# Filler products cut into quarters beside the attention scores, with drains and a new table

## The chip, the cores and the metric

The kernel runs on one core of a Trainium2 chip. The metric is the device time of one execution in microseconds, the median of several. A core has five engines that work side by side and wait for each other by semaphores: TensorE (PE in the profile, its weight loads PEld), VectorE (DVE), ScalarE (ACT), GpSimd (POOL) and SyncE (SP), which issues most DMAs. TensorE has an array of 128 by 128 cells; a matmul can be given a part of it, here 32 of its columns with all 128 rows ("128*32" in the profile) or 32 of its rows with all 128 columns ("32*128").

## What is computed

Two layers, each an attention block and an MLP block on x of 2048 by 512, with the same weights in both layers:

```python
def _A_ref(x, wqkv, wo):            # H = 32 heads of Dh = 16
    qkv = (x @ wqkv).reshape(B, S, 3, H, Dh).transpose(2, 0, 3, 1, 4)
    q, k, v = qkv[0], qkv[1], qkv[2]
    scores = jnp.einsum("bhqd,bhkd->bhqk", q, k) * (Dh ** -0.5)
    p = _softmax(scores, axis=-1)
    o = jnp.einsum("bhqk,bhkd->bhqd", p, v)
    return o.transpose(0, 2, 1, 3).reshape(B, S, D) @ wo

def _B_ref(x, w1, w2):              # Dff = 1792
    return jnp.maximum(x @ w1, 0) @ w2

x = x + _A_ref(_layernorm(x), A_wqkv, A_wo)
x = x + _B_ref(_layernorm(x), B_w1, B_w2)
# and both once more
```

The output is bfloat16. Most of the work is 2 x 32 x 2048 x 2048 exponentials.

## The kernel before

**Slots.** The scores come in blocks of 128 keys by 512 queries of one head. Four heads lie side by side in a tile of keys and queries, each in 32 of the 128 partitions; the number of such a group, g from 0 to 3, is the row group of the array in which the block's scores are computed. A slot takes three blocks (`W = 3`), of three different groups where it can, writes their scores with three matmuls (L2231) into one of two PSUM buffers `ps_s` of three banks, and has ScalarE take the exponential of all three, or of two (L2249). There are 1366 slots, one exponential instruction each. Where two are taken, VectorE makes the third block's exponential from an integer word (L1750), and GpSimd adds a constant to two such blocks at a time, up and down (L1811); the block is then summed in three parts.

**Columns.** Each exponential block is multiplied by the values (L1404), into one of two accumulators, `ps_o` or `ps_f`. Head g writes 32 partitions, so these matmuls take 128 rows and 32 columns, and four of them with different g run side by side, a round. `v_round` (L1488) issues a round; where it has no block for some of the four groups of columns, it may put a filler cell there (`grid_column`, L501).

**Fillers.** All else that TensorE has to do, the projections and both MLP matmuls, is cut into groups of products (`mm_group`, L681). A product multiplies 128 rows by 128 columns by 512, and a group adds 4 of them into a bank (14 in the second MLP matmul), which VectorE then reads. A group of this kind is a *grid*: each product is four cells of 32 columns (`grid_cell`, L463, its matmul on L467), and a full unit (`grid_unit`, L484) issues four. The bank is whichever of `ps_o` and `ps_f` the sums of the attention do not hold.

**The order.** The program is written out in order by a planner in Python. It keeps a clock for each engine (`now_pe`, `now_dve`, `now_pool`, `now_act`), advances it by a fixed cost for each instruction (`MM = 216`, `SWITCH = 105` for a change between rows and columns, and so on, in ns), and fills each slot up to a limit (L2190) with rounds and filler units: `pace` says how many filler units a slot ought to do, `owed` how many it is behind, `margin` how long before ScalarE needs them the scores ought to be done. Only the order of instructions comes out of this; the engines still wait for each other by semaphores. `take_unit` (L2021) picks the blocks of a slot. `rule` holds the planner's settings, and `RULES` changes some of them from a given slot on. `STARTS` forces or forbids a slot's third for VectorE, `MORE` adds to what is owed, `SLIP` moves a slot's limit.

At the head of a slot's scores stands

```python
        for _ in range(times):
            pe_run("s", 1, s_ready, TUCK[now[0][0]["w"]])
            for a, (sg, kb, g) in sorted(zip(place, now), key=in_turn):
```

so that the planner counts one matmul's time for all three.

Of the kernel before, what the change touches and what calls it, by code (L numbers as in the profile page):

```python
# [26 lines left out]
def kernel(  # L27
# [10 lines left out]
    nc = tc.nc  # L38
# [13 lines left out]
    QS = 512  # L52
# [18 lines left out]
    GROUP = 2  # L71
# [17 lines left out]
    SMALL, W1, TRANSPOSE = (600.0, 1600.0), (430.0, 3000.0), (1400.0, 3600.0)  # L89
# [6 lines left out]
    STARTS, MORE, SLIP = {13: 0, 16: 1, 40: 0, 23: 1, 30: 0, 33: 0, 56: 0, 53: 0, 54: 1, 47: 0, 103: 1, 127: 1, 141: 1, 184: 1, 252: 1, 254: 0, 313: 0, 342: 0, 353: 0, 344: 1, 370: 1, 382: 1, 419: 1, 451: 0, 453: 1, 456: 0, 444: 0, 508: 0, 509: 1, 538: 0, 532: 1, 547: 0, 566: 1, 578: 0, 585: 1, 592: 0, 642: 1, 654: 0, 646: 0, 641: 1, 670: 0, 696: 1, 682: 0, 719: 0, 715: 1, 728: 1, 737: 1, 772: 0, 819: 1, 834: 0, 857: 0, 844: 1, 855: 0, 854: 1, 873: 0, 886: 1, 905: 1, 918: 1, 938: 1, 929: 0, 976: 0, 1000: 0, 1006: 1, 1001: 0, 1025: 0, 1031: 1, 1092: 0, 1128: 1, 1151: 1, 1166: 1, 1172: 0, 1250: 0, 1260: 0, 1266: 1, 1263: 0, 1340: 0, 1326: 0, 1364: 0, 1362: 0, 1366: 0, 1371: 0}, {9: -1.0, 13: 2.0, 7: 2.0, 38: 1.0, 39: 2.0, 32: 2.0, 52: 2.0, 41: -1.0, 48: 1.0, 126: 1.0, 153: 2.0, 187: -1.0, 204: 2.0, 221: -1.0, 237: 1.0, 229: -1.0, 264: 2.0, 265: -1.0, 266: 1.0, 300: 2.0, 281: 1.0, 285: 1.0, 308: 1.0, 320: 2.0, 318: -1.0, 327: -1.0, 355: 2.0, 378: -1.0, 371: 1.0, 372: 2.0, 388: 2.0, 396: -1.0, 391: -1.0, 437: 1.0, 495: 2.0, 538: 2.0, 543: 2.0, 574: 2.0, 603: 2.0, 659: 1.0, 684: -1.0, 685: 1.0, 711: -1.0, 807: 1.0, 804: 2.0, 813: -1.0, 828: 1.0, 836: 2.0, 832: 2.0, 855: 2.0, 879: 2.0, 861: -1.0, 862: -1.0, 896: 1.0, 897: 1.0, 899: 2.0, 956: -1.0, 948: 1.0, 961: 2.0, 987: -1.0, 1008: 1.0, 1035: -1.0, 1079: 1.0, 1089: 1.0, 1100: -1.0, 1099: -1.0, 1110: 2.0, 1164: 1.0, 1263: -1.0, 1267: 2.0, 1277: 2.0, 1299: 1.0, 1336: 2.0, 1365: -1.0, 1375: 1.0, 1371: 2.0}, {3: 120.0, 56: -200.0, 102: 60.0, 133: -200.0, 175: -200.0, 194: 120.0, 184: -200.0, 196: 120.0, 259: 60.0, 245: 60.0, 241: -200.0, 321: -200.0, 325: -200.0, 322: 60.0, 357: -200.0, 370: -200.0, 366: 120.0, 377: -200.0, 384: -200.0, 385: -200.0, 390: 120.0, 419: 120.0, 434: 216.0, 436: 120.0, 435: 60.0, 497: -200.0, 517: 60.0, 523: 60.0, 530: -200.0, 521: -200.0, 551: -200.0, 549: 60.0, 559: 216.0, 574: -200.0, 634: 60.0, 666: -200.0, 691: 216.0, 692: 60.0, 689: -200.0, 718: -200.0, 722: -200.0, 726: -200.0, 740: 120.0, 818: 120.0, 828: 60.0, 825: 60.0, 822: -200.0, 891: -200.0, 922: 60.0, 932: -200.0, 931: 120.0, 946: 60.0, 951: -200.0, 945: 60.0, 1011: 216.0, 1013: -200.0, 1002: 216.0, 1034: 60.0, 1062: 216.0, 1064: 120.0, 1067: 60.0, 1097: 60.0, 1114: 60.0, 1131: 120.0, 1220: -200.0, 1218: 60.0, 1242: 216.0, 1279: 60.0, 1289: -200.0, 1294: 216.0, 1296: 216.0, 1312: 60.0, 1307: -200.0, 1308: 60.0, 1323: 216.0, 1353: -200.0, 1361: -200.0, 1365: -200.0, 1370: -200.0}  # L96
# [6 lines left out]
        "haste": 2.0, "margin": 130.0, "join": -1.0, "room": 0, "keep": 2, "wide": 1, "share": 4,  # L103
    }
    RULES = {1: {'rounds': 3, 'hold': 2, 'closing': 3, 'fill': 2000.0}, 21: {'young': 5}, 41: {'easy': 1.0, 'keep': 1}, 61: {'old': 3, 'spare': 6, 'rounds': 4, 'fill': 3000.0, 'over': 200.0, 'young': 6, 'pressed': 6, 'closing': 6}, 101: {'least': 0.5, 'spare': 20, 'margin': 160.0, 'far': 4}, 121: {'near': 8, 'pressed': 2, 'soon': 1400.0, 'old': 4}, 141: {'keep': 2, 'late': 4.0, 'ahead': 8.0, 'unit': 360.0}, 161: {'pressed': 6, 'hold': 3, 'spare': 6, 'least': 0.8, 'far': 4, 'soon': 2000.0, 'haste': 1.6, 'near': 4}, 181: {'wide': 1, 'haste': 3.0}, 201: {'hold': 4, 'backlog': 3000.0}, 221: {'keep': 3, 'easy': 1.4, 'haste': 2.0, 'far': 2}, 241: {'haste': 3.0, 'full': 4}, 261: {'margin': 100.0}, 281: {'late': 3.0}, 301: {'late': 99.0, 'least': 0.5, 'unit': 400.0, 'easy': 1.0, 'keep': 2, 'young': 5, 'pace': 1.0, 'full': 3}, 321: {'keep': 3, 'easy': 2.0}, 341: {'young': 3}, 361: {'haste': 2.0}, 401: {'young': 6, 'unit': 360.0}, 421: {'pace': 1.0, 'slack': 1300.0, 'over': 0.0, 'eager': 0, 'partial': 3, 'backlog': 2200.0, 'closing': 3, 'cap': 3.0}, 441: {'pace': 1.15, 'young': 6, 'rounds': 4, 'keep': 2, 'calm': 3.0, 'far': 2, 'soon': 1400.0, 'unit': 320.0}, 461: {'slack': 1300.0, 'fill': 2000.0, 'closing': 3, 'unit': 360.0}, 481: {'unit': 400.0, 'soon': 2000.0, 'rounds': 4, 'late': 4.0, 'eager': 0, 'least': 0.5, 'fill': 2000.0, 'haste': 1.6}, 541: {'late': 2.0, 'least': 0.8}, 561: {'keep': 2, 'near': 10, 'margin': 100.0, 'hold': 2}, 581: {'ahead': 12.0, 'closing': 6, 'slack': 800.0, 'full': 5}, 601: {'ahead': 8.0, 'cap': 6.0}, 661: {'near': 12, 'ahead': 12.0, 'closing': 3, 'pace': 1.15}, 701: {'spare': 10}, 721: {'haste': 2.0, 'rounds': 4, 'near': 10, 'over': 0.0, 'pace': 1.3, 'eager': 1, 'keep': 2, 'young': 5}, 761: {'hold': 4, 'partial': 3, 'pace': 0.7, 'cap': 3.0, 'closing': 0, 'wide': 2, 'join': -1.0, 'near': 10}, 801: {'late': 99.0}, 821: {'eager': 1, 'calm': 1.2}, 841: {'keep': 2, 'cap': 3.0, 'least': 0.8, 'share': 4, 'backlog': 2200.0, 'room': 0, 'near': 6, 'haste': 1.3}, 861: {'backlog': 3000.0}, 881: {'share': 2}, 901: {'full': 3}, 921: {'eager': 1, 'rounds': 4, 'least': 0.5, 'partial': 3, 'margin': 60.0, 'haste': 1.6, 'full': 3, 'pace': 1.5}, 941: {'over': 60.0, 'late': 99.0}, 961: {'partial': 2, 'near': 12, 'cap': 10.0, 'far': 3, 'easy': 1.2, 'slack': 1300.0, 'soon': 1000.0, 'full': 3}, 981: {'rounds': 3, 'backlog': 2200.0}, 1021: {'wide': 0, 'cap': 6.0}, 1061: {'over': 200.0, 'spare': 10}, 1081: {'spare': 20, 'haste': 1.3, 'over': 120.0, 'slack': 300.0, 'easy': 1.6, 'backlog': 1500.0, 'room': 0, 'pace': 0.85}, 1101: {'soon': 1400.0, 'unit': 320.0}, 1121: {'far': 2, 'slack': 300.0, 'fill': 3000.0, 'ahead': 1.0, 'calm': 2.0, 'haste': 2.0, 'hold': 2, 'cap': 3.0}, 1161: {'unit': 400.0, 'far': 3}, 1241: {'near': 12, 'haste': 1.3, 'keep': 2, 'eager': 0}, 1261: {'full': 5}, 1301: {'keep': 2, 'cap': 3.0}, 1321: {'rounds': 3, 'room': 8}, 1341: {'fill': 2000.0, 'spare': 10}, 1361: {'fill': 2000.0, 'over': 60.0, 'hold': 3, 'unit': 400.0, 'eager': 0, 'ahead': 8.0, 'calm': 3.0, 'pressed': 6}}
# [232 lines left out]
    mode = [None]  # L338
    grid = [None]
# [46 lines left out]
    def pe_run(kind, units, ready=0.0, extra=0.0):  # L386
        start = pe_start(kind, ready)
        now_pe[0] = start + units * MM + extra
        mode[0] = kind
        streams.append((start, now_pe[0]))  # L390
# [51 lines left out]
    def start_group(g):  # L442
# [8 lines left out]
        if g["grid"]:  # L451
            n = len(g["grid"]["mms"])
            grid[0] = dict(
                g["grid"], b=bank(), ready=ready, cols=[deque(range(n)) for _ in range(4)],
                begun=[False] * 4,
            )
            cur.extend((1.0, grid_unit, ready if n == 0 else 0.0, "f") for n in range(n))
            return
# [4 lines left out]
    def grid_cell(c, g):  # L463
        G = grid[0]
        lhsT, rhs = G["mms"][c]
        cols = slice(32 * g, 32 * g + 32)
        nc.tensor.matmul(  # L467
            G["b"][cols], lhsT[:, cols], rhs, start=not G["begun"][g], stop=not G["cols"][g],
            tile_position=(0, 32 * g), skip_group_check=True,
        )  # L470
        G["begun"][g] = True

    def grid_settle():
        G = grid[0]
        n = max(len(x) for x in G["cols"])
        while len(cur) > n:
            cur.pop()
# [6 lines left out]
    def grid_unit():  # L484
# [3 lines left out]
        grid_settle()  # L488

# [20 lines left out]
    def do_piece():  # L510
        c, fn, ready, kind = cur.popleft()
        pe_run(kind, c, ready)
        fn()
        owed[0] -= c
# [12 lines left out]
    def fill_pe(limit, floor=0.0, most=99):  # L527

        done = 0
        while owed[0] > floor and done < most:  # L530
            limit_now = limit if owed[0] < 5.0 or not hurry[0] else now_pe[0] + 1000.0
# [286 lines left out]
    def ln_rows(tag, tt, n, i):  # L818
# [11 lines left out]
        if i == n - 1:  # L830
# [26 lines left out]
            for k in range(n):  # L857
                task(
                    420, lambda k=k: apply(k),
# [1636 lines left out]
```

## Time and profile before

| | |
|---|---|
| median of 3 runs | 1368.37 us (1368.16 to 1368.6) |
| the profiled execution | 1367.16 us |
| its span, first to last instruction | 1365.4 us |
| TensorE's granted clock | 1.0 |
| exponentials, L2249, ScalarE | 1319.0 us busy |
| filler cells, L467, TensorE | 5000 matmuls |
| GpSimd busy | 58% |

The page of the profile gives each engine's busy time and its share of the span, then the chain of work that ended last. Matmuls are pipelined: a matmul's record is longer than the time after which the next can start, so a busy share near 100% says that work follows on work, not that the array is used to its peak. Timelines give the start, the length, the engine, the line, the operation, what is written from what, and how many such instructions are merged. A "q" behind an engine's name (PEldq) is its sequencer.

### The profile page before, as it was taken

The numbers are of one execution on the slowest core, as the hardware profiler recorded it, in microseconds if no ns is written. First come the engines' busy times: TensorE is split into PE (matmuls) and PEld (weight loads), VectorE is DVE, ScalarE is ACT, GpSimd is POOL, SyncE is SP. The second block draws the span as 40 slices with busy tenths as digits, with TensorE's granted clock in tenths as the row PEclk, the third lists the DMA queues.
The fourth block names the chain that finished last, engine by engine and source line by source line (L and its number), as shares of the span: only waits on it lengthen the run. The fifth ranks groups of instructions, "written<-read, shape, count | busy, mean of one in ns | idle before, by whom it ended". The sixth has DMA issues, their size and how long they took to land.

```text
span 1365.4 us, 49106 instructions
## 1 busy us (share of the span) xinstructions
PE 1327.1 (97%) x20780; PEld 468.5 (34%) x20782; DVE 1161.8 (85%) x2024; ACT 1333.1 (98%) x1437; POOL 789.0 (58%) x1324
## 2 busy tenths in 40 slices
PE   8999999999999999999999999999999999999998
PEld 3222222222222222222222222222234444545665
DVE  7898889878998789997899877998888888988883
ACT  8999999999999999999999999999999999999994
POOL 3357766666666566675466654565446565666440
PEclk9999999999999999999999999999999999999999
DMA  6200112112024120321203100002312401324112
GB/s 152 66 2 18 26 33 42 42 43 41 11 52 107 33 57 14 95 53 41 49 21 90 29 29 13 26 16 49 102 43 49 113 21 41 78 45 99 31 39 37
DMA packets 166669, 66.63 MB, mean 49 GB/s; under 512 B 137617, under 2 KB 161617, under 8 KB 166449
## 3 DMA queue, kind: packets, MB, share of 16 engines
q1 hardware_dynamic: 159920, 57.89, 17.5%
q0 software_dynamic: 5568, 5.15, 2.0%
q8 instruction: 162, 2.65, 0.8%
q10 hardware_dynamic: 960, 0.46, 0.1%
q14 instruction: 59, 0.48, 0.1%
HBM read 38.80 MB, written 4.19 MB: 31 GB/s over the span
## 4 chain that ended last, share of the span: by engine, by line
PE 56%; ACT 33%; DVE 8%; issue 2%; DMA 1%; POOL 0%; SPq 0%; POOLq 0%; DVEq 0%; ACTq 0%
PE ps_s L2231 19%; ACT e L2249 15%; PE ps_f L1404 9%; PE ps_o L1404 9%; PE ps_o L467 8%; PE ps_f L467 7%; ACT xx L2249 7%; DVE words L1750 3%; ACT w L2249 3%; ACT wv L2249 2%; ACT val L2249 2%; ACT ktl L2249 1%; ACT words L2249 1%; ACT ktp L2249 1%; PE ps_o L716 1%
## 5 line engine op out<-in xcount | busy, mean ns | idle before, releaser
L2249 ACT ACTIVATE e<-ps_s 128x1024 bf16<-128x1024 f32 (+1 forms) x627 | 695.2, 1190 | 5.9 <-PE ps_s L2231 2.2
L1750 DVE TENSOR_SCALAR words<-ps_s 128x512 int16<-128x512 f32 x864 | 580.8, 685 | 94.9 <-PE ps_s L2231 81.5
L1811 POOL INT64_ADD words<-words x581 | 356.0, 622 | 258.9 <-DVE words L1750 205.4
L2231 PE MATMUL ps_s<-q,ktp 32*128 32x512 bf16 (+2 forms) x4110 | 478.2, 331 | 14.9 <-ACT e L2249 7.5
L2231 PEld LDWEIGHTS <-ktp 32*128 32x128 bf16 x4393 | 151.5, 91 | 452.1 <-issue 445.0
L2249 ACT ACTIVATE xx<-ps_s 128x1024 bf16<-128x1024 f32 x283 | 300.9, 1128 | 1.4 <-PE ps_s L2231 1.1
L2231 PE MATMUL ps_s<-q,ktl 32*128 32x256 bf16 (+2 forms) x1359 | 197.6, 289 | 0.9 <-ACT ktp L2249 0.3
L1404 PEld LDWEIGHTS <-vaug 128*32 128x32 bf16 x4686 | 116.4, 95 | 150.0 <-issue 130.7
L2249 ACT ACTIVATE w<-ps_s 128x1024 bf16<-128x1024 f32 x111 | 118.1, 1106 | 0.0
L1404 PE MATMUL ps_f<-e,vaug 128*32 128x512 bf16 (+2 forms) x830 | 111.6, 322 | 0.4 <-DVE q L977 0.2
L1404 PE MATMUL ps_o<-e,vaug 128*32 128x512 bf16 (+2 forms) x768 | 105.9, 335 | 0.3 <-DVE ht L1236 0.2
L1750 DVE TENSOR_SCALAR xx<-ps_s 128x512 int16<-128x512 f32 x128 | 86.4, 683 | 16.4 <-PE ps_s L2231 14.0
L1404 PE MATMUL ps_o<-words,vaug 128*32 128x512 bf16 (+2 forms) x647 | 92.1, 348 | 0.7 <-DVE u L1260 0.3
L1404 PE MATMUL ps_f<-words,vaug 128*32 128x512 bf16 (+2 forms) x559 | 89.5, 373 | 0.8 <-DVE vaug L953 0.5
L1404 PEld LDWEIGHTS <-val 128*32 128x32 bf16 x2744 | 73.3, 96 | 44.9 <-issue 34.8
L2231 PEld LDWEIGHTS <-ktl 32*128 32x128 bf16 x1359 | 61.4, 92 | 56.6 <-issue 55.0
L1404 PE MATMUL ps_o<-words,vscaled 128*32 128x512 bf16 (+2 forms) x514 | 78.7, 331 | 1.5 <-POOL words L1811 1.1
L1811 POOL INT64_ADD words<-xx x83 | 50.7, 620 | 49.0 <-DVE xx L1750 29.6
L2249 ACT ACTIVATE val<-ps_s 128x1024 bf16<-128x1024 f32 x67 | 73.6, 1129 | 0.0
L467 PE MATMUL ps_o<-w,ht 128*32 128x512 bf16 x896 | 73.0, 383 | 0.0
L2249 ACT ACTIVATE wv<-ps_s 128x1024 bf16<-128x1024 f32 x65 | 71.7, 1123 | 0.6 <-PE ps_s L2231 0.5
L1404 PE MATMUL ps_o<-xx,vaug 128*32 128x512 bf16 (+1 forms) x325 | 70.2, 382 | 0.6 <-DVE vaug L1258 0.5
(318 smaller groups left out, 2651.4 us busy)
## 6 DMA issues: line engine op xcount, KB each, us to landing
w<-in_B_w_dram SPq DMA_DIRECT2D x144, 128.0 KB
w<-in_B_w_dram SPq DMA_DIRECT2D x35, 256.0 KB
q<-xn SPq DMA_DIRECT2D x38, 64.0 KB
wv<-in_A_wqkv_dram SPq DMA_DIRECT2D x8, 256.0 KB
away<-xx SPq DMA_DIRECT2D x8, 256.0 KB
xx<-away SPq DMA_DIRECT2D x8, 256.0 KB
out_dram<-xx SPq DMA_DIRECT2D x15, 128.0 KB
xx<-in_A_x_dram SPq DMA_DIRECT2D x14, 128.0 KB
```

The source lines that it names most:

```text
L467: nc.tensor.matmul(G["b"][cols], lhsT[:, cols], rhs, start=not G["begun"][g], stop=not G["cols"][g], tile_position=(0, 32 * g), skip_group ...
L716: nc.tensor.matmul(out[cols], lhsT[:, cols], rhs, start=i % k == 0, stop=i % k == k - 1, tile_position=(0, 32 * g), skip_group_check=True,)
L1404: nc.tensor.matmul((ps_f, ps_o)[sg["bank"]][32 * g : 32 * g + 32, 0 : sg["w"]], values[:, 4 * sg["T"] + g, 2 * e : 2 * e + 32], rhs, start ...
L1750: first = nc.vector.tensor_scalar(out=words[which][:, half * QS : (half + 1) * QS], in0=src, scalar1=EXP_BIAS, scalar2=THIRD, op0=ALU.add, ...
L1811: ins = nc.gpsimd.int64_add(of(part).bitcast(I64), of("lin").bitcast(I64), by)
L2231: score = nc.tensor.matmul(b[:, a : a + sg["w"]], kt[32 * g : 32 * g + 32, kc : kc + P], q_home(sg["q"])[32 * g : 32 * g + 32, sg["e"], 0 ...
L2249: ex = nc.scalar.activation(out=eb[:, 0 : place[m]], in_=b[:, 0 : place[m]], func=ACTF.Exp, scale=1.0 / (LOG2E * UNIT),)
```

## The change

A filler product may now be cut the other way, into four quarters of 32 rows, each with all 128 columns, that add into the same bank. Just ahead of the first of a slot's scores, `beside_scores` looks for a row group that none of the slot's blocks uses, and issues one quarter there, so that it runs beside the scores. It opens a group for this if none is open. A new product is cut only if at least `rest` times the pace (at most 1) products remain uncut in the group, and only before any or after all of the four column groups have begun. There is at most one quarter between two changes of mode. Every quarter of a group but its first has a `drain` of TensorE ahead of it. When a group's columns are done and quarters are left, they wait up to `hang` slots for scores to go beside and are then issued in a phase of their own. `wish` keeps a row group free by having `take_unit` avoid it. The planner counts no time for a quarter beside scores nor for its drain.

Three of the planner's costs change: 420 to 400 for applying a normalization, (1400, 3600) to (1260, 3000) for a transpose by DMA, and `quick` from 150 to 67 plus the same term. `STARTS`, `MORE`, `SLIP` and `RULES` are replaced whole. In the new table `rest` is 3.0 at first, 2.0 from slot 81, 6.0 from 181, 6.0 from 481, 4.0 from 661 and 3.0 from 1221; `margin` is 130 at first and 60 from slot 161 on (before: 130, 160 from 101, 100 from 261, 60 from 921); `hang` is 2, and 1 from 1101 to 1360; `wish` is 1, 2 from 341, 1 from 541, 0 from 741 and 1 from 961. `STARTS` has 54 forbidden and 33 forced starts, before 45 and 36.

```diff
...
-    SMALL, W1, TRANSPOSE = (600.0, 1600.0), (430.0, 3000.0), (1400.0, 3600.0)
+    SMALL, W1, TRANSPOSE = (600.0, 1600.0), (430.0, 3000.0), (1260.0, 3000.0)
...
     def pe_run(kind, units, ready=0.0, extra=0.0):
         start = pe_start(kind, ready)
+        switches[0] += MODE[mode[0]] != MODE[kind]
...
     def grid_settle():
         G = grid[0]
         n = max(len(x) for x in G["cols"])
+        if n:
+            while len(cur) > n:
+                cur.pop()
+            return
+        n = sum(len(x[1]) for x in G["rows"])
+        if G["since"] is None:
+            G["since"] = slot[0]
+            cur.clear()
+            cur.extend((1.0, grid_row, 0.0, "s") for _ in range(n))
...
+    def grid_row(g=None):
+
+        G = grid[0]
+        x = next(x for x in G["rows"] if g is None or g in x[1])
+        g = x[1][0] if g is None else g
+        x[1].remove(g)
+        G["at"] = switches[0]
+        G["rows"] = [x for x in G["rows"] if x[1]]
+        lhsT, rhs = G["mms"][x[0]]
+        rows = slice(32 * g, 32 * g + 32)
+        if G["last"]:
+            nc.tensor.drain()
+        nc.tensor.matmul(
+            G["b"], lhsT[rows], rhs[rows], start=not G["begun"][0],
+            stop=not G["rows"] and not any(G["cols"]),
+            tile_position=(32 * g, 0), skip_group_check=True,
+        )
+        G["last"] = True
+        G["begun"] = [True] * 4
+        grid_settle()
+
+    def wished():
+
+        G = grid[0]
+        rows = [g for x in G["rows"] for g in x[1]] if G else []
+        return rows[:1] if rule["wish"] and rows and (rule["wish"] > 1 or G["since"] is not None) else []
+
+    def beside_scores(used):
+
+        idle = [g for g in range(4) if g not in used]
+        if two[0] or not idle:
+            return
+        open_grid()
+        G = grid[0]
+        if G is None or G["ready"] > now_pe[0] - MM or G["at"] == switches[0]:
+            return
+        g = next((g for g in idle if any(g in x[1] for x in G["rows"])), None)
+        if g is None:
+            fresh = min(G["cols"], key=len)
+            if len(fresh) - 1 < rule["rest"] * min(pace, 1.0) or len(set(G["begun"])) > 1:
+                return
+            g, c = idle[0], fresh[-1]
+            for x in G["cols"]:
+                x.remove(c)
+            G["rows"].append((c, [0, 1, 2, 3]))
+        owed[0] -= 0.25
+        grid_row(g)
...
     def do_piece():
         c, fn, ready, kind = cur.popleft()
         pe_run(kind, c, ready)
+        owed[0] -= 0.25 if kind == "s" else c
         fn()
-        owed[0] -= c
...
         while owed[0] > floor and done < most:
+            if cur and cur[0][3] == "s" and slot[0] < grid[0]["since"] + rule["hang"]:
+                return done
...
-                    420, lambda k=k: apply(k),
+                    400, lambda k=k: apply(k),
...
-        quick = 150 + 0.2591 * GROUP * QS
+        quick = 67 + 0.2591 * GROUP * QS
...
-            banked.append(take_unit(heads(banked)))
+            banked.append(take_unit(heads(banked) + wished()))
...
             pe_run("s", 1, s_ready, TUCK[now[0][0]["w"]])
+            if not scores:
+                beside_scores({x[2] for x in now})
...
```

More of the change, by code (lines that the diff above doesn't have):

```diff
@@ L102 @@
         "rounds": 4, "partial": 3, "far": 3, "young": 3, "old": 5, "slack": 1300.0, "eager": 0,
[L103 removed]
+        "haste": 2.0, "margin": 130.0, "join": -1.0, "room": 0, "keep": 2, "wide": 1, "share": 4, "rest": 3.0, "hang": 2, "wish": 1,
     }
[L105 removed]
@@ L338 @@
     mode = [None]
+    switches = [0]
     grid = [None]
@@ L454, in start_group @@
                 g["grid"], b=bank(), ready=ready, cols=[deque(range(n)) for _ in range(4)],
-                begun=[False] * 4,
+                begun=[False] * 4, rows=[], since=None, at=-1, last=False,
             )
@@ L467, in grid_cell @@
         nc.tensor.matmul(
-            G["b"][cols], lhsT[:, cols], rhs, start=not G["begun"][g], stop=not G["cols"][g],
+            G["b"][cols], lhsT[:, cols], rhs, start=not G["begun"][g],
+            stop=not G["cols"][g] and not G["rows"],
             tile_position=(0, 32 * g), skip_group_check=True,
```

3 lines of the change are left out of this document (2 added, 1 removed).

## The prediction

> **What bounds the kernel now.** The page's head comes first: how full each engine is, and which engines carry the chain that ended last.
>
> ```profile
> span 1365.4 us, 49106 instructions
> PE 1327.1 (97%) x20780; PEld 468.5 (34%) x20782; DVE 1161.8 (85%) x2024; ACT 1333.1 (98%) x1437; POOL 789.0 (58%) x1324
> ...
> PE 56%; ACT 33%; DVE 8%; issue 2%; DMA 1%; POOL 0%; SPq 0%; POOLq 0%; DVEq 0%; ACTq 0%
> ```
>
> TensorE and ScalarE are both full, and the chain changes between them: over half of it is TensorE. Two full engines that feed each other in 1366 slots call for one slot, so the timeline around 602 us is read next (start, length, engine, line).
>
> ```profile
> 601.45 1.14 ACT L2249 ACTIVATE e<-ps_s 128x1024 bf16<-128x1024 f32 x1
> ...
> 601.89 0.39 PE L2231 MATMUL ps_s<-q,ktp 32*128 32x512 bf16 x3
> ...
> 602.21 0.40 PE L1404 MATMUL ps_f<-xx,vaug 128*32 128x512 bf16 x4
> ...
> 602.37 1.13 ACT L2249 ACTIVATE wv<-ps_s 128x1024 bf16<-128x1024 f32 x1
> ...
> 602.43 0.39 PE L467 MATMUL ps_o<-xnT,w 128*32 128x512 bf16 x4
> 602.75 0.10 PEld L2231 LDWEIGHTS <-ktp 32*128 32x128 bf16 x3 [0.42 <-issue]
> 602.76 0.39 PE L2231 MATMUL ps_s<-q,ktp 32*128 32x512 bf16 x3
> ...
> 603.27 1.15 ACT L2249 ACTIVATE xx<-ps_s 128x1024 bf16<-128x1024 f32 x1
> ```
>
> Three things are to be seen. A column round (four matmuls side by side, one for each group of 32 columns) takes 602.43 - 602.21 = 0.22 us. A change between columns and rows costs more: 602.75 - 602.43 = 0.32 us from the start of the last round to the scores' weight load, so 0.10 us beyond the round, while the round's own modelled end is 602.43 + 0.39 = 602.82. And the exponentials start every 0.90 to 0.92 us, about 0.1 us after the scores' modelled end (602.76 + 0.39 = 603.15, then 603.27). TensorE is hardly ahead. How much it ever waits for ScalarE, and ScalarE for it, stands in the view of the exponentials' line:
>
> ```profile
> its engine sat idle before it (us, times) until:
>   PE ps_s L2231: 5.0, 12
> ...
> who waited for it (us, times):
>   PE ps_s L2231: 16.5, 62
> ```
>
> The scores waited for an exponential 62 times, 16.5 us in all. That is all the cover that TensorE has over 1365 us: work added to it is hidden up to 16.5 us (plus some 0.1 us once after each catch-up) and then shows in full. By the same rule, work taken from it is worth having.
>
> **What the change takes away.** A filler product over 128 rows is cut into four quarters of 32 rows. One quarter goes beside a slot's scores, which use at most three row groups. It costs no round of its own, because matmuls of different groups start within 0.01 us of each other in the rows above. So each placed quarter saves 0.22 / 4 = 0.054 us of TensorE. The matmuls and loads stay as many: four 128*32 cells become four 32*128 quarters.
>
> How many are placed is not in the trace and must be estimated. The view of the filler's line, in six stretches (stretch, length, PE busy and its count), gives the stock:
>
> ```profile
> 0.00:50.00 50.00, 17.73 (x240) 5.71 (x240) 1.00 0.57 137
> 50.00:300.00 250.00, 62.01 (x780) 15.73 (x780) 1.00 0.13 31
> 300.00:700.00 400.00, 135.77 (x1700) 32.59 (x1700) 1.00 0.20 47
> 700.00:1100.00 400.00, 131.29 (x1652) 34.48 (x1648) 1.00 0.20 50
> 1100.00:1300.00 200.00, 40.69 (x500) 10.35 (x496) 1.00 0.24 53
> 1300.00:1365.00 65.00, 9.28 (x128) 2.94 (x128) 1.00 0.21 38
> ...
> L467 PE MATMUL ps_o<-w,ht x896: 376/379/392, 288.1 to 1283.7; 128*32 128x512 bf16 x180
> ...
> L467 PE MATMUL ps_f<-w,ht x728: 376/379/392, 277.4 to 1343.0; 128*32 128x512 bf16 x182
> ```
>
> The stretches add up to 5000 cells, 1250 products, a little under one for each slot. The last two rows are the second MLP matmul: 1624 / 56 = 29 groups of 14 products. The remaining 3376 cells make about 210 groups of four.
> - Groups of 14: with the table's "rest" of 6 (slots 181 to 660) a new product may be cut while six others would stay. A slot uses about one product by columns and one quarter, so cuts come with 14 and about 9 left: 8 quarters; with a rest of 3 or 4 (elsewhere) a third cut, 12 quarters. 29 groups give 232 to 348; I take 290.
> - Groups of four: only an untouched group may be cut, and only where rest times the pace is at most 3. By the table that excludes most of slots 181 to 660. Between none and all (840 quarters) I take one group in four, 52 groups, 208 quarters, because the search for a free bank falls on the scores only now and then.
>
> That makes 500 quarters (ends 230 and 900) and 500 x 0.054 = **27 us of TensorE saved**.
>
> **What the change adds: drains.** From the second quarter of a group on, a drain goes ahead of the quarter. Behind it in TensorE's queue stand the quarter's load and matmul and then the three scores of the slot. ScalarE's exponential, VectorE's third of the scores and GpSimd's additions wait for those. Groups of 14 have drains on all but one of 8 to 12 quarters, groups of four on three of four: 260 + 156, about 415.
>
> No drain stands in the middle of before's trace. At its end, TensorE has one behind matmuls in flight:
>
> ```profile
> L2491 PEldq DRAIN  x2: 13/285/557, 1361.4 to 1364.8; - x2
> ...
> 1360.91 1.04 PE L2339 MATMUL ps_s<-w,ht 128*128 128x256 bf16 x8
> ...
> L467 PEldq EVENT_SEMAPHORE  x19: 51/51/51, 32.1 to 1045.2; - x19
> ```
>
> It began at 1361.4 and took 0.557 us, so it ended at 1361.96 (within 0.05, by the rounding); the matmuls ahead of it end at 1360.91 + 1.04 = 1361.95. The other one, with nothing in flight, took 0.013. So a drain holds the sequencer to the modelled end of the last matmul. In the slot above that end is 602.82, whereas the scores' loads start at 602.75 today. Hence:
> - the low end of a drain's price is 0.07 us, the part of the last round that the change of groups does not wait for;
> - behind it the queue is empty. The nearest row for a sequencer's step is the 0.051 us above. Eight instructions (four loads, four matmuls) then come one by one. Today three loads and three matmuls start within 0.01 us because they stood ready. A rate of issue is bounded only by 41,562 matmuls and loads in 1327 us, 0.032 us each, so between 0 and 0.26 us. The high end is 0.07 + 0.05 + 0.26 = 0.38 us.
>
> I take 0.07 + 0.05 + 0.04 = 0.16 us, near the low end, because the two terms with rows of their own make most of it and the issue is likely far faster than an average that includes waiting. 415 x 0.16 = **66 us added**, 29 and 158 at the ends. The column cells behind the scores are issued during the scores' 0.32 us, which hides that.
>
> **The rest.** The new costs for a normalization (400), a transpose (1260, 3000) and a scaling (67) only change where the order by hand puts things; no instruction and no DMA is added. The table decides which slots give a third to VectorE and how near the fillers go to the scores. Its margin is 60 from slot 161 on, where before it was 160 to slot 260 and 100 to slot 920: there the plan leaves 0.04 to 0.1 us less cover for each score. That speaks against the change, since 0.16 us does not fit into it. What a new order is worth by itself no row says; I bound it by 5 us either way and take 0.
>
> **The sum.** 66 added, 27 saved, up to 16 hidden in waits for ScalarE: 66 - 27 - 16 = 23 to 66 - 27 = 39, middle 31. The profiled execution took 1367.2 us (span 1365.4 and 1.8 around it), so 1398.2; the median of the runs is 1.2 above it: **1399 us**.
>
> **The rivals.**
> - *The drain falls into the pause that is there* (faster). Place: the 0.10 us between a column round and the scores. Were the array empty at the end of that pause, a drain would add next to nothing. Price: the 27 us saved stay, of which about half arrive, since TensorE has 56% of the chain and ScalarE 33%: 1368 - 14 = **1354 us**. It decides below (27 + 16) / 415 = 0.10 us for a drain. For it: the low end is 0.07. Against it: the drain at the end held until the modelled end of its matmuls, 0.07 us after the pause would be over here, and the restart comes on top.
> - *Leftover quarters go alone.* When a group's columns are done and no slot offers the row group within "hang" slots, a quarter takes a phase of its own, 0.22 us for 0.054 us of work, and its bank is kept from the next group. If a quarter of the 500 end so, 125 x 0.22 = 27 us on top: **1426 us**. For it: only two banks, and each quarter has to meet its own group among the idle ones. Against it: the next units are chosen so as to leave that group idle ("wish").
> - *It hardly happens.* If the conditions (an untouched group, a free bank, an operand ready) are rarely met, some 100 quarters, the drains' 13 us and the 5 us saved nearly vanish in the waits, and the new order decides: **1368 us**, 5 either way.
>
> The Trainium skill bears on the first rival: "TensorEngine Tiling (Array Packing)", Key Properties, says that a change of tiling mode drains TensorE. By that rule a drain ahead of the scores repeats what the change does anyhow, the 66 us would be 0, and the sum 27 us less than before. The pause of 0.10 us at each change agrees with some drain there; but it ends 0.07 us ahead of the modelled end, so I give the rule alone no more than that rival's chance.
>
> **How the numbers follow.** Forecast 0.52, drain in the pause 0.25, quarters alone 0.15, hardly any 0.08 (of it 0.03 faster, 0.03 within, 0.02 slower). A measurement of this kernel can tell about 0.2%, some 3 us. Faster 0.25 + 0.03 = 0.28, within 0.2% 0.03, slower 0.52 + 0.15 + 0.02 = 0.69. The cases have both signs, so the range runs from inside the first rival to above the second: 1350 to 1440. 1440 is 415 drains at 0.28 us less 27 and 16 (1368 + 73 = 1441), between the value taken and the high end. The forecast's own range is 1380 to 1432 (drains of 0.13 to 0.22 us, with 27 saved and 16 or none hidden).
>
> **What would show it.** A new line of 32*128 matmuls into ps_o and ps_f counts the quarters (500), and TensorE's DRAIN rows count the drains (415). Where a drain stands, the last column round to the scores should take about 0.48 us instead of 0.32, and the exponential behind it should start late; idle time of ScalarE ahead of its exponentials should rise from under 10 us to tens. If that interval stays at 0.32, the step on the drain's price is wrong and the first rival holds. If ScalarE's idle time does not grow although the interval does, the plan has cover that I did not see. If the counts are far off, the estimate of the placed quarters is wrong, and with it both terms.

## The result, and the profile after

The changed kernel takes 1390.7 us, median of 4 runs (1389.7 to 1391.3), against 1368.3 for before: a ratio of 1.0162, 95% interval 1.0149 to 1.0174. It is 22 us slower; the forecast was 31 us. Of the first experiment below, one execution of four took 3706.7 us, the one that was profiled, so its time is the median of the other three and nothing is read from its profile.

The head of the page of the profile after (its own execution: 1391.3 us):

```profile
span 1389.5 us, 49309 instructions
...
PE 1334.4 (96%) x20773; PEld 465.4 (33%) x20775; DVE 1169.2 (84%) x2035; ACT 1346.8 (97%) x1437; POOL 794.7 (57%) x1334
...
PE 65%; ACT 24%; DVE 6%; issue 4%; DMA 1%; SPq 0%; POOL 0%; POOLq 0%; DVEq 0%
```

TensorE's share of the chain goes from 56 to 65%, and "issue", time in which the engine waits for nothing that the profile shows, from 2 to 4%; the time in a drain is of that kind. The same order without drains (all columns, below) has 63% and 2%: TensorE's larger share comes with the order, the issue with the drains. ScalarE has the same 1437 instructions (ten more exponentials of two blocks and ten fewer of three, some 4 us less work), yet it is busy 13.7 us longer: it is held up without having more to do.

The two new lines of the program, the drain (L513) and the quarter's matmul (L514), in the views of these lines:

```profile
L513 PEldq DRAIN  x187: 250/917/1568, 56.5 to 1363.4; - x187
```

```profile
L514 PE MATMUL ps_f<-w,ht x108: 371/382/385, 289.7 to 1363.9; 32*128 32x512 bf16 x108
L514 PE MATMUL ps_o<-w,ht x96: 371/382/385, 275.6 to 1306.0; 32*128 32x512 bf16 x96
L514 PE MATMUL ps_o<-wo,ot x8: 382/382/385, 1283.6 to 1342.9; 32*128 32x512 bf16 x8
L514 PE MATMUL ps_o<-wv,xnT x4: 382/382/384, 55.4 to 58.6; 32*128 32x512 bf16 x4
L514 PE MATMUL ps_f<-xnT,wkq x4: 382/382/384, 99.4 to 102.6; 32*128 32x512 bf16 x4
```

There are 220 quarters (55 products) and 187 drains, not 500 and 415. The groups of 14 hold 204 quarters, the groups of four only the 16 of the last three rows. The drain's own length (0.9 us) says nothing: its record begins when the sequencer takes it up, while the columns ahead of it are still running.

What a drain does is to be seen in a slot, here from 446.6 us on:

```profile
446.63 0.62 PE L469 MATMUL ps_f<-w,ht 128*32 128x512 bf16 x8
...
447.34 0.38 PE L514 MATMUL ps_f<-w,ht 32*128 32x512 bf16 x1
...
447.35 0.39 PE L2295 MATMUL ps_s<-q,ktp 32*128 32x512 bf16 x3
...
447.78 1.02 ACT L2313 ACTIVATE xx<-ps_s 128x1024 bf16<-128x1024 f32 x1
...
447.89 0.61 PE L469 MATMUL ps_f<-w,ht 128*32 128x512 bf16 x8
...
448.59 0.38 PE L514 MATMUL ps_f<-w,ht 32*128 32x512 bf16 x1
...
448.60 0.39 PE L2295 MATMUL ps_s<-q,ktp 32*128 32x512 bf16 x3
...
449.06 1.45 ACT L2313 ACTIVATE e<-ps_s 128x1536 bf16<-128x1536 f32 x1 [0.26 <-PE ps_s L2295]
```

Eight column cells are two rounds; the second starts 0.22 us after the first, at 446.85 and 448.11, and the quarters start 0.49 and 0.48 us behind it (0.32 in before). Over all records of the trace the median is 0.475 us with a drain and 0.312 without one: **0.163 us for a drain**. Taken apart, the drain ends 0.037 us after the modelled end of the last round, and the quarter starts 0.059 us after that. The first of the three scores follows the quarter by 0.003 to 0.006 us, so a fourth matmul beside them costs next to nothing. At most 5 of the 220 quarters stand without scores beside them.

ScalarE's waits, in the view of the exponentials' line:

```profile
its engine sat idle before it (us, times) until:
  PE ps_s L2295: 12.9, 39
  PE ps_o L1466: 2.6, 3
  PE ps_f L1466: 1.3, 4
who waited for it (us, times):
  PE ps_s L2295: 12.6, 49
```

The last row is TensorE's cover: 16.5 us in before, and still 12.6. The first is only 8 us more than before, and a poor measure of what was lost. The exponential of two blocks has a record of 1.02 us, but the next can start 0.904 us after it started; the first 0.12 us of each delay lies under that record and isn't called idle. Counted from start to start beyond 0.904 us (1.331 for three blocks), the exponentials are late by 68 us in all after and by 39 before. In the 186 slots that have a drain and a following exponential it is 0.180 us each, in the other 1179 slots 0.029.

### The profile page after: what moved, and what is told of

Read it like the earlier page. It is cut to its first block, busy times and chain, and to the rows that moved or that the text cites. A ratio compares the mean times of both kernels' runs of the same rounds, so it can differ in the third digit from the quotient of the medians.

```text
span 1389.5 us, 49309 instructions
## 1 busy us (share of the span) xinstructions
PE 1334.4 (96%) x20773; PEld 465.4 (33%) x20775; DVE 1169.2 (84%) x2035; ACT 1346.8 (97%) x1437; POOL 794.7 (57%) x1334
## 4 chain that ended last, share of the span: by engine, by line
PE 65%; ACT 24%; DVE 6%; issue 4%; DMA 1%; SPq 0%; POOL 0%; POOLq 0%; DVEq 0%
PE ps_s L2295 18%; ACT e L2313 15%; PE ps_o L1466 12%; PE ps_f L1466 11%; PE ps_f L469 8%; PE ps_o L469 8%; ACT xx L2313 3%; PE ps_f L514 3%; PE ps_o L514 2%; DVE words L1812 2%; ACT val L2313 1%; ACT ktl L2313 1%; PE ps_o L778 1%; ACT w L2313 1%; ACT words L2313 1%
## 5 line engine op out<-in xcount | busy, mean ns | idle before, releaser
L2313 ACT ACTIVATE e<-ps_s 128x1024 bf16<-128x1024 f32 (+1 forms) x833 | 871.2, 1125 | 9.3 <-PE ps_s L2295 5.4
L1812 DVE TENSOR_SCALAR words<-ps_s 128x512 int16<-128x512 f32 x788 | 531.0, 685 | 104.9 <-PE ps_s L2295 96.0
L1873 POOL INT64_ADD words<-words x508 | 309.4, 617 | 217.9 <-DVE words L1812 185.0
L2313 ACT ACTIVATE xx<-ps_s 128x1024 bf16<-128x1024 f32 x182 | 192.3, 1077 | 2.0 <-PE ps_s L2295 1.5
L1466 PE MATMUL ps_o<-e,vaug 128*32 128x512 bf16 (+2 forms) x946 | 130.5, 343 | 0.7 <-DVE q L1039 0.4
L1466 PE MATMUL ps_f<-e,vaug 128*32 128x512 bf16 (+2 forms) x949 | 125.9, 338 | 0.6 <-issue 0.2
L1812 DVE TENSOR_SCALAR xx<-ps_s 128x512 int16<-128x512 f32 x130 | 87.7, 683 | 20.5 <-PE ps_s L2295 17.4
L1873 POOL INT64_ADD xx<-words x98 | 60.9, 623 | 43.7 <-DVE words L1812 30.6
L1466 PE MATMUL ps_f<-words,vscaled 128*32 128x512 bf16 (+2 forms) x506 | 69.2, 320 | 0.0
L2313 ACT ACTIVATE vaug<-ps_s 128x1024 bf16<-128x1024 f32 (+1 forms) x63 | 64.8, 1049 | 1.3 <-PE ps_s L2295 0.9
L1466 PEld LDWEIGHTS <-vscaled 128*32 128x32 bf16 x1558 | 57.3, 96 | 24.6 <-issue 16.7
```

The lines of the kernel that those rows point to most:

```text
L1466: nc.tensor.matmul((ps_f, ps_o)[sg["bank"]][32 * g : 32 * g + 32, 0 : sg["w"]], values[:, 4 * sg["T"] + g, 2 * e : 2 * e + 32], rhs, start ...
L1812: first = nc.vector.tensor_scalar(out=words[which][:, half * QS : (half + 1) * QS], in0=src, scalar1=EXP_BIAS, scalar2=THIRD, op0=ALU.add, ...
L1873: ins = nc.gpsimd.int64_add(of(part).bitcast(I64), of("lin").bitcast(I64), by)
L2313: ex = nc.scalar.activation(out=eb[:, 0 : place[m]], in_=b[:, 0 : place[m]], func=ACTF.Exp, scale=1.0 / (LOG2E * UNIT),)
```

## The experiments

**The order of after, with one thing changed at a time.** In the next four kernels the planner runs as in after, so that every other instruction keeps its place; only what is written out differs. The first leaves out the quarters behind drains and the drains.

```diff
-        if G["last"]:
-            nc.tensor.drain()
-        nc.tensor.matmul(
+        if not G["last"]:
+            nc.tensor.matmul(
...
```

> The changed kernel in its own order; the 187 quarters that have a drain ahead of them are left out together with their drains (33 quarters without a drain stay), so this part of the filler products isn't computed. Theory, the drains cost it: 187 x 0.16 us = 30, of which up to 16 may hide, so 1361 to 1375 us, and the waits in the slots that had a drain fall from 0.18 us to the 0.03 of the other slots, which points to the low end, about 1362. Rival, the new table's tighter order costs it: 1385 or more, since the order is kept.

Measured: 1360.3 us, ratio to before 0.9933 (0.9917 to 0.995).

The second keeps the drains and leaves out the quarters behind them.

```diff
         if G["last"]:
             nc.tensor.drain()
-        nc.tensor.matmul(
+        else:
+            nc.tensor.matmul(
...
```

> The same order; the 187 drains stay, the quarters behind them are left out. Theory, the drains: as slow as the changed kernel, 1389 to 1392 us. Rival, the fourth matmul beside the scores is what slows them: as fast as with both left out, near 1362.

Measured: 1389.2 us, 1.0143 (1.0127 to 1.0158). 187 drains cost 1389.2 - 1360.3 = 28.9 us, 0.155 each, with no quarter behind them; all 187 quarters together add the last 1.5 us to after (2.6 by the ratios to before), which the intervals don't tell from nothing. The page shows it too: matmuls are fewer than in after by the 187, the engines otherwise as busy.

```profile
span 1388.2 us, 48935 instructions
...
PE 1331.6 (96%) x20586; PEld 464.0 (33%) x20588; DVE 1169.3 (84%) x2035; ACT 1346.5 (97%) x1437; POOL 794.9 (57%) x1334
```

In the third a quarter is written out only where its slot lies two or more behind the last one of its group (112 quarters, 79 drains); the fourth has the same quarters, and a wait in place of each drain. The first diff is against after, the second against the third kernel (`exp_of` holds each slot's exponential).

```diff
-        if G["last"]:
-            nc.tensor.drain()
-        nc.tensor.matmul(
+        if not G["last"] or slot[0] >= G["last"] + 2:
+            if G["last"]:
+                nc.tensor.drain()
+            nc.tensor.matmul(
...
+            G["last"] = slot[0]
```

```diff
-            if G["last"]:
-                nc.tensor.drain()
-            nc.tensor.matmul(
+            quarter = nc.tensor.matmul(
...
+            if G["last"]:
+                tc.add_manual_dep(
+                    quarter.ins, exp_of[G["last"]],
+                    mybir.DependencyInfo(mybir.DependencyClass.Sync, mybir.DependencyReason.DATA),
...
             G["last"] = slot[0]
```

> The same order; of the quarters behind a drain only those are kept that come two slots or more after the last one kept: 79 drains and 112 quarters are left, the other 108 quarters are left out without their drains. Theory, the drains: 79 of 187 drains, so 79 x 0.15 = 12 us above the version with neither, 1373 to 1376. Rival, the order: no less than 1385.

> As e3 with the same 112 quarters, but in place of each of the 79 drains the quarter waits for the exponential of the slot in which the quarter before it was issued, two slots or more ago, which the scores wait for anyhow. Theory, the drains: the wait is over when it is reached, so as fast as with both left out, about 1362 us, although 79 quarters more run beside scores. Rival, the quarters: slower than that by what a fourth matmul costs, up to 79 x 0.1 = 8 us.

Measured: 1371.15 us (1.0018, 1.0009 to 1.0027) with drains and 1357.8 us (0.9914, 0.9897 to 0.993) with waits. The 79 drains cost 13.4 us, 0.17 each. The wait is on the exponential of a slot two or more back, which is behind the scores that stand behind the earlier quarter; it orders the two quarters without holding anything up: over this trace the median from a round to a quarter behind it is 0.312 us, as from a round to scores alone. In the profile of the fourth ScalarE is busy 18.6 us less than in after:

```profile
span 1356.7 us, 48906 instructions
...
PE 1321.6 (97%) x20665; PEld 464.6 (34%) x20667; DVE 1167.1 (86%) x2035; ACT 1328.2 (98%) x1437; POOL 793.2 (58%) x1334
```

**Drains in the kernel before.** Does the price belong to the order of after, or to the place in a slot? Two kernels put drains into before's own order.

```diff
             pe_run("s", 1, s_ready, TUCK[now[0][0]["w"]])
...
+            if not scores and no % 7 == 0 and no >= 55:
+                nc.tensor.drain()
```

> The kernel before with nothing of the change in it but the drains: 188 of them, each between the last column product of a slot and that slot's scores, in every seventh slot from the 55th. No quarter exists and the order is that of before. My theory: a drain costs 0.15 us wherever TensorE goes over from column products to scores, whatever the order and whether a quarter follows; 188 x 0.15 = 28 us, so 1397 us. The rival: the 28 us of the drains in the order after come from that order, which packs the slots that hold them more tightly; here the drains would fall into slots that have room, and cost 5 us or less, so 1373 us or less.

```diff
...
     def grid_unit():
+        if round_in[0] == slot[0] and slot[0] >= 55 and slot[0] - round_in[1] >= 5:
+            nc.tensor.drain()
+            round_in[1] = slot[0]
+        round_in[0] = slot[0]
```

> The kernel before with 161 drains at another place: in the middle of a slot's column products, between two rounds of filler, where TensorE doesn't change from columns to rows. My theory: a drain costs the time in which the engine empties and starts again, less what the place pays anyhow. Two rounds in a row start about 0.22 us apart and a round's modelled length is 0.39 us; with a drain between them the second starts 0.39 + 0.04 + 0.06 = 0.49 us after the first, 0.27 us late; ahead of the scores 0.10 us of that is paid already by the change from columns to rows. So 161 x 0.27 = 43 us, less some 10% that hides: about 1407 us. The rival: a drain is an instruction of a fixed price, 0.16 us wherever it stands: 161 x 0.15 = 24 us, 1392 us.

Measured: 1391.2 us (1.0161, 1.0144 to 1.0178), 0.116 us for each of the 188 drains ahead of scores; and 1408.2 us (1.0286, 1.027 to 1.0301), 0.241 for each of the 161 within the columns. Both rivals fall: outside the new order a drain ahead of scores costs three quarters as much (0.116 for 0.155; my 0.15 was too high), and the price depends on the place. The timelines around 600 us show a run of three rounds, 12 cells, first in the kernel with drains ahead of scores, then in the one with drains within the columns:

```profile
600.30 0.83 PE L467 MATMUL ps_o<-xnT,w 128*32 128x512 bf16 x12
601.06 0.39 PE L2233 MATMUL ps_s<-q,ktp 32*128 32x512 bf16 x3
```

```profile
600.05 1.11 PE L469 MATMUL ps_f<-xnT,w 128*32 128x512 bf16 x12
601.09 0.39 PE L2237 MATMUL ps_s<-q,ktp 32*128 32x512 bf16 x3
```

The same three rounds are 0.28 us longer with a drain in them, and the scores behind them start 1.04 us after the first instead of 0.76. Over all records the filler rounds start 0.212 us apart, and 0.486 with a drain between them: 0.274 us. The drain's end (0.036 us after the modelled end) and the restart (0.060) are the same at both places; what differs is what the place pays anyhow. At a change from columns to scores the pause of 0.10 us is part of the emptying, so 0.274 - 0.10 = 0.17 is left, which is the 0.163 to 0.165 seen there.

The Trainium skill, "TensorE: Matmul & The Clock Gate", in "Step-by-step: what each phase is for", says that the last wavefront of a matmul runs out while the next is already being fed, and in "Single matmul latency" it gives 166 ns at full clock for what a single matmul takes beyond the time of its columns. The trace agrees nearly: a round's record ahead of these drains is 0.39 us (its end is modelled) and the next round starts 0.21 us after its start, so a drain makes 0.18 us visible; with the 0.036 and the 0.060 that is 0.27.

**The table without quarters.**

```diff
     def beside_scores(used):
+        return
```

> The kernel after with its new table and constants, but no quarter is ever taken from the columns: all filler products are whole columns, there is no drain, and the planner makes its order anew. Everything is computed. My theory: the table was fitted to an order that holds the quarters, and is worth nothing by itself; the planner's own clock ends 10.7 us later than for before (1346.5 against 1335.8), so 1378 us. The rival: the new table is the better one by itself, and the 8 us that the planner gains come from it rather than from the quarters: 1360 us.

Measured: 1387.4 us, 1.013 (1.0115 to 1.0145). The table belongs to its order: as soon as a planned quarter is missing, the planner writes another order, and a worse one. My size was off by 9 us, for a reason that the next runs made plain.

**New tables.** I searched the planner's tables further, once without quarters and once with quarters and waits, by the planner's clock at the end of the last exponential.

> Everything is computed and no quarter is cut: the constants of before, and a table found by a further search on the planner's own clock, which ends at 1323.9 us for it (before: 1335.8). The offset from the planner's end to the measured time was 32.6 us for before, 38 to 41 for orders that the table was not fitted to. My theory: a fitted order keeps the small offset, 1323.9 + 32 = 1356 us, so a better table is worth 12 us without any quarter. The rival: the last microseconds that such a search wins are the planner's cover, which the chip takes back, and the time stays above 1362 us.

> Everything is computed. The constants of after, 156 quarters; a quarter that is two slots or more behind the last one of its group waits for the exponential of that one's slot in place of a drain (104 such waits), and 19 drains are left where the slots lie closer. The table is found by a search as for the run without quarters; the planner's clock ends at 1320.3 us. My theory: quarters are nearly free and waits cost nothing, so 1320.3 + 32 + 19 x 0.15 = 1355 us, faster than before and than after, and level with the run without quarters (1356), within 3 us: the quarters save 156 x 0.054 = 8 us of TensorE, of which the planner's clock shows 4 and the 19 drains take 3 back. The rival: the waits, or the load that a quarter puts beside the scores, cost what the drains did, and the time is 1365 us or more.

Besides its table, the kernel with quarters and waits differs from after in the edit below, and it issues no quarter beside scores in the slot just behind the last one of its group.

```diff
         apart = G["last"] and slot[0] >= G["last"] + 2
         if G["last"] and not apart:
             nc.tensor.drain()
...
+        if apart:
+            tc.add_manual_dep(
+                quarter.ins, exp_of[G["last"]],
...
```

The third has drains alone in the order of the second (`if G["last"]: nc.tensor.drain()`, no wait).

> The same order as the run with 104 waits and 19 drains, instruction for instruction, everything computed, but each of the 104 waits is a drain again: 123 drains. My theory: 104 x 0.15 = 16 us above that run, so 1371 us. The rival: where the drains are spread over more slots, at most one in two of a run of slots, the plan has time to catch up between them, and they cost less than 0.05 us each: 1360 us.

Measured: 1390.1 us (1.0152, 1.0138 to 1.0165), 1411.3 us (1.0305, 1.0291 to 1.0319) and 1421.2 us (1.0386, 1.0372 to 1.04). A part of the output of the last two is wrong, for a cause that stays open. No matmul of a product is missing: their 4836 cells and 156 quarters are together the 4992 filler cells in the trace of before (the 5000 above counts eight at the edges of its stretches twice). So I read their times as those of the full work. My theory on the absolute times fell, by 34, 56 and 50 us, far beyond its rival. The view of the exponentials' line without quarters shows where:

```profile
L2324 ACT ACTIVATE e<-ps_s x650: 640/1156/1766, 10.8 to 1335.3; 128x1024 bf16<-128x1024 f32 x133, 128x1536 bf16<-128x1536 f32 x30
```

The last exponential starts at 1335.3 us, 5 us earlier than in before (1340.1), but the span is 1387.6: 52 us of work follow it, where before has 25. The search had pushed filler groups behind the point at which it stopped the clock: 224 filler cells start behind the last exponential, 60 in before. The planner's TensorE clock at the end of everything would have told:

| kernel | planner's last `now_pe` | span | difference |
|---|---|---|---|
| before | 1348.5 | 1365.4 | 16.9 |
| after | 1339.5 | 1389.5 | 50.0 |
| after's order, half the quarters, waits | 1339.5 | 1356.7 | 17.2 |
| no quarters | 1369.9 | 1386.9 | 17.0 |
| new table, no quarters | 1370.2 | 1387.6 | 17.4 |
| new table, waits, 19 drains | 1388.3 | 1406.5 | 18.2 |

The row of after stands out because the planner doesn't count the drains: by its clock the change was 9 us better than before.

What these three runs do tell is the difference between waits and drains in one order: 104 drains for waits cost 9.9 us, 0.095 each. That is more than the rival's 0.05 and less than my 0.15. Why it is less isn't shown: at most every second slot of a run has a drain here, but so it is with the 79 drains above, which cost 0.17 each; and the executions of these two kernels scatter by 4 to 5 us.

**What the quarters save, and a version without drains.** Both of these keep the order of after and compute everything. In the first, each of the 55 cut products is issued whole; in the second, 18 of them keep their quarters, in slots two or more apart and with waits. `quarters[0]` counts the planned quarters; `KEPT`, in the second only, and `COLUMNS` say which of them become a quarter and where a whole product goes.

```diff
-        if G["last"]:
-            nc.tensor.drain()
-        nc.tensor.matmul(
...
+        c = COLUMNS.get(quarters[0])
+        if c is not None:
+            lhsT, rhs = G["mms"][c]
+            for n in range(4):
+                cols = slice(32 * n, 32 * n + 32)
+                nc.tensor.matmul(
+                    G["b"][cols], lhsT[:, cols], rhs, start=not wrote[n],
...
+        c = KEPT.get(quarters[0])
+        if c is not None:
+            lhsT, rhs = G["mms"][c]
+            quarter = nc.tensor.matmul(
+                G["b"], lhsT[rows], rhs[rows], start=not wrote[0],
...
+            if "kept" in G:
+                tc.add_manual_dep(
+                    quarter.ins, exp_of[G["kept"]],
...
```

> The order of after, everything computed, and no quarter and no drain: each of the 55 products that after cuts into quarters is issued whole, as a round of four column cells, ahead of the scores of the slot in which its last quarters stood. This measures what the quarters save and what the new order is worth without them. My theory: 55 rounds x 0.216 = 12 us of TensorE come on top of the order without drains (1361 us), and 8 to 12 us of them arrive: 1369 to 1373 us, so that the new order by itself is worth about nothing and what after gained it gained by the quarters. The rival: rounds in these slots hide, the order by itself is the better one: 1364 us or less.

> The order of after, everything computed, no drain: 18 of the 55 products keep their four quarters, in slots of the original places that lie two or more apart, each quarter behind the first waiting for the exponential of the slot of the one before; the other 37 products are rounds of column cells as in the run with all 55. My theory: a quarter beside the scores is free and so is the wait, so it is 18 x 0.216 = 3.9 us less than with all 55 as columns: 1366 us, just below before (1368 to 1369). The rival: the waits hold the scores that stand behind them, and it is no faster than with all 55 as columns.

Measured: 1366.1 us, 0.9982 (0.9973 to 0.9991), and 1363.2 us, 0.9963 (0.995 to 0.9975). So the new order by itself is about 2 us better than before's; of 55 rounds' 12 us only some 6 arrive (1366.1 against the 1360.3 of the first experiment, where 33 quarters stand beside scores and 187 are left out), less what those 187 cost; and of the 18 rounds' 3.9 us, 2.9. The second kernel is faster than both before and after, than before by 0.4%. The first also shows how much cover this order has without a drain, in the view of its exponentials' line:

```profile
who waited for it (us, times):
  PE ps_s L2303: 12.4, 48
```

That is no more than the 12.6 us of after: the drains used up none of it.

In the timeline of the second a quarter with a wait (L533, the second of its group) starts 0.32 us after the round ahead of it, as scores alone do:

```profile
444.26 0.39 PE L474 MATMUL ps_f<-w,ht 128*32 128x512 bf16 x4
...
444.58 0.38 PE L533 MATMUL ps_f<-w,ht 32*128 32x512 bf16 x1
444.58 0.39 PE L2324 MATMUL ps_s<-q,ktp 32*128 32x512 bf16 x3
```

**Not tried.** Quarters of neighbouring slots with nothing between them: nothing in the program would order their additions into one bank, and no run here shows whether that is needed. A wait of a quarter on the one in the slot just before, short of that slot's exponential: no engine but TensorE has seen the end of it by then.

**The account.** Ratios to before, each taken beside its own runs of before, times 1368.3 us. By the ratios' intervals a change is known to within 1 to 3 us, so the last one is not clear of noise.

| step | kernel | us | change |
|---|---|---|---|
| | before | 1368.3 | |
| new order, products whole | all columns | 1365.8 | -2.5 |
| 33 quarters beside scores, 187 left out | left out | 1359.1 | -6.7 |
| 187 drains | drains only | 1387.9 | +28.7 |
| 187 quarters beside scores | after | 1390.5 | +2.6 |

## Why the prediction came out as it did

- *What bounds it* held. Of the 187 x 0.163 = 30.5 us that the drains hold TensorE, 28 to 29 arrive. The cover of 16 us that I let hide part of it hid next to nothing: TensorE still waits 12.6 us, and 12.4 in the same order without drains, so it is the order that took the rest of the 16.5. Quarters come four or eight in a row of slots, and a wait elsewhere may not help such a row; that this is the reason isn't shown, since the 79 drains two or more slots apart cost 0.17 each too. Where the drains were spread over before's slots, a quarter to a third of the price did hide ahead of scores (0.116 of 0.165), and an eighth within the columns (0.241 of 0.274).
- *The price of a drain* was the step that carried the forecast: 0.16 predicted, 0.163 measured. Its three terms were shifted among themselves. The drain ends 0.037 us past the modelled end, so the tail is 0.11 rather than 0.07; the restart is 0.06 (0.05 predicted); the issue of the eight instructions behind it is 0.01 at most (0.04 predicted).
- *The counts* failed: 220 quarters and 187 drains for 500 and 415. In groups of 14 I took 8 to 12 quarters for each of 29 groups; it was 4 or 8. In groups of four I took one group in four out of 210; it was 4 groups. The search for a bank did what I took it to do: the planner opens 48 groups of four at a slot's scores, nearly one in four. The step that failed is the reading of the table. `rest` times the pace refuses 44 of the 48, all in slots 181 to 1220, where `rest` is 6 or 4; I had excluded most of 181 to 660 and nothing behind.
- *The saving* was 0.054 us for a quarter by the round that it spares. That is right as TensorE's time, but it arrives in part: 2.9 of 3.9 us for 18 products, some 6 of 12 for 55, less up to 2.6 that 187 quarters add beside scores. With the count, the term is 4 to 7 us in place of 27.
- *The order by itself*, 0 within 5, is -2.
- *The sum*: drains 30 for 66, saving 4 to 7 for 27, hidden 2 for 8 in the middle, order -2 for 0. The counts were wrong by the same factor in two terms of opposite sign; with the right counts my own formula would have said 30 - 12 - 8 = 10 us, too little by 12. That 31 came near 22 owes something to errors that cancel. The sign and the mechanism do not: they hung on the drain's price.
- *The rivals.* A drain that falls into the pause needed under 0.10 us; the pause covers 0.10 of 0.274 and no more. The rule of the Trainium skill behind it ("TensorEngine Tiling (Array Packing)", Key Properties), that a change of mode drains TensorE, is thus borne out by a part only: the change of mode waits 0.10 us, and an explicit drain there still costs 0.163. Leftover quarters in phases of their own are 5 at most. "It hardly happens" was the nearest in count, but 187 drains don't vanish in the waits.
- *The signs that I named*: the interval of 0.48 us came (0.475). ScalarE's idle time went from 9.2 to 16.8 us, not to tens; the loss stands in its start times instead.

## What to carry to other kernels

Price a barrier by what the engine would have overlapped at that place, not by its record: here the emptying of the array plus a restart, less the pause that is there anyhow. Where an order between two instructions is all that is wanted, a wait on something that lies behind the first and is long done costs nothing; spread the two far enough apart that such a thing exists. And before a planner's clock is used to choose, let it stop at the end of all the work and count what it leaves out, the drains here.

## What the runs showed of the hardware

- A matmul in the idle fourth row group starts 0.003 to 0.006 us before the three scores and delays them by no more than that.
- TensorE takes up the next instruction 0.06 us after a drain's end, and a drain ends 0.036 to 0.038 us after the modelled end of the last matmul, alike within columns and ahead of a change to rows.
- Exponentials of 0.904 us from start to start have records of 1.02: a delay below 0.12 us shows in no idle row.
